# q before k in the first block, finer first transfers and a tile copied by two engines, in a fused attention and gMLP kernel

## The chip, the cores and the metric

The kernel runs on one core of a Trainium2 chip. The metric is the device time of one execution in microseconds (us). TensorE is called PE in the profile, VectorE DVE, ScalarE ACT, GpSimd POOL and SyncE SP.

## What is computed

The reference adds three things to one another for an input of 2048 tokens by 512 features in bf16: the input itself, a sliding local attention over eight earlier positions two tokens apart (32 heads of 16 features), and a gated MLP whose gate mixes all 2048 tokens by a matrix. Both branches start from the same layer norm of x.

```python
xn = _layernorm(x, axis=-1)
return x + _A_ref(xn, A_wqkv, A_wo) + _B_ref(xn, B_w_in, B_w_sp, B_b_sp, B_w_out)

# A: q, k, v = xn @ wqkv; logits over offsets 0, 2, ..., 14; softmax; weighted sum of v; @ wo
# B: z = gelu(xn @ w_in); z2 = layernorm(second half)
#    g = w_sp @ z2 + b_sp; (first half * g) @ w_out
```

## The kernel before

The tokens are cut into 16 tiles of 128. Tile i = 4 * tb + j belongs to block j, so that a block holds four tiles, one from each quarter tb of the sequence. In the code t0, i1, i2 and i3 are the tile numbers of blocks 0 to 3. Everything is kept in SBUF: `xall` holds x of all tiles and is normalised in place, `xnT` holds the normalised x with features on the partitions, `wqk` the weights of q (s = 0) and of k (s = 1), each in four chunks `kc` of 128 input features.

Each engine works through its instructions in the order in which the program text issues them: the schedule is written out by hand. The start of the kernel, with which the change deals, is plain code; after it a long string ORDER of tokens gives the order of all that follows (the gMLP's matmuls `z`, the remaining q and k, the products of the attention and so on).

At the start each tile goes through these steps:

- `ln_stats` (DVE): mean and variance by a statistics instruction and an aggregate. `ln_sqrt` (ACT): the square root of the variance plus epsilon, for one column or for a slice of several tiles' columns. `ln_recip` (DVE): its reciprocal. `ln_apply` (DVE): subtract and multiply in place. `ln_tile` is `ln_recip` and `ln_apply` of one tile.
- a transpose to `xnT`, in one of two ways: `tr` has PE write four 128 by 128 transposes to a PSUM tile `pt`, which `tr_copy` has ACT copy to `xnT`; `tr_dma` has SP issue a DMA transpose. Block 0 and two tiles of block 1 go by PE, the other tiles by DMA.
- q and k: `qk_part(pq, j, m, b0, b1)` has PE multiply the weights by tiles b0 to b1 of block j into the PSUM tile `pq`. m = 0 and 1 are the two halves of q, m = 2 and 3 those of k. `qk_copy` has ACT cast the result to SBUF.

The PSUM tiles of q, k and z come from one pool of three, `ps_mm`, so that a fourth tile waits until the first has been read. The `pt` tiles come from a pool of two, `ps_aux`.

x and the weights arrive by DMA. SP and ACT issue the first transfers: halves of the first two tiles of x on both, the other two tiles of block 0 on ACT, and on SP the q weights in two transfers of two chunks, x of block 1 in two transfers of two tiles, the k weights in one, then x of blocks 2 and 3 and the weights of z. In the built program all transfers share eight completion semaphores in turn.

Of the kernel before, what the change touches and what calls it, by code (L numbers as in the profile page):

```python
# [15 lines left out]
P = 128  # L16
# [3 lines left out]
TB = 4  # L20
TBS = 512
C = D // P
# [48 lines left out]
def kernel(  # L71
# [13 lines left out]
    V = nc.vector  # L85
# [3 lines left out]
    SP = nc.sync  # L89
# [3 lines left out]
    xblk = x2.rearrange("(b j p) d -> j p b d", b=TB, j=4)  # L93
# [9 lines left out]
    xall = r_x[:, 0:4 * TB * D].rearrange("p (j b d) -> p j b d", j=4, b=TB)  # L103
# [33 lines left out]
    xnT = sb.tile([P, C, S], BF16, name="xnT")  # L137
# [31 lines left out]
    def load_wqk(E, s, k0=0, k1=C):  # L169
        E.dma_start(wqk[:, s, k0:k1],  # L170
                    A_wqkv[:, s * D:(s + 1) * D].rearrange("(k p) f -> p k f", p=P)[:, k0:k1])
# [3 lines left out]
        load_x0(A, tb, 1)  # L175
    for tb in range(2, TB):
        A.dma_start(xall[:, 0, tb], xblk[0][:, tb])
    load_wqk(SP, 0, 0, 2)
    load_wqk(SP, 0, 2, 4)
    SP.dma_start(xall[:, 1, 0:2], xblk[1][:, 0:2])  # L180
    load_wqk(SP, 1)
    SP.dma_start(xall[:, 1, 2:4], xblk[1][:, 2:4])
    for j in range(2, 4):
        SP.dma_start(xall[:, j], xblk[j])
    SP.dma_start(w_z2[:], B_w_in[:, FH:F].rearrange("(k p) f -> p k f", p=P))
# [20 lines left out]
    def ln_stats(i, parts=1):  # L206
        j, tb = i % 4, i // 4
        w = D // parts
        for h in range(parts):
            V.bn_stats(stats[:, i, 6 * h:6 * h + 6], xall[:, j, tb, w * h:w * h + w])  # L210
        V.bn_aggr(mv[:, i, :], stats[:, i, 0:6 * parts])

    def ln_sqrt(sl):
        A.activation(rstd[:, sl], mv[:, sl, 1], ACT.Sqrt, bias=eps_t[:])

    def ln_recip(sl):
        V.reciprocal(rstd[:, sl], rstd[:, sl])

    def ln_apply(i):
        j, tb = i % 4, i // 4  # L220
        V.tensor_scalar(xall[:, j, tb, :], xall[:, j, tb, :], mv[:, i, 0:1], rstd[:, i:i + 1],
                        ALU.subtract, ALU.mult)

    def tr(i):
        j, tb = i % 4, i // 4
        pt = ps_aux.tile([P, C, P], BF16, name="pt", tag="aux")
        for c in range(C):
            PE.transpose(pt[:, c, :], xall[:, j, tb, c * P:(c + 1) * P], ident[:])  # L228
        return pt

    def tr_copy(i, pt, c0=0, c1=C):
        A.copy(xnT[:, c0:c1, i * P:(i + 1) * P], pt[:, c0:c1, :])

    def tr_dma(i):
        j, tb = i % 4, i // 4
        SP.dma_start_transpose(xnT[:, :, i * P:(i + 1) * P], xall[:, j, tb, :])
# [70 lines left out]
    def qk_part(pq, j, m, b0, b1, ccs=(0, 1), p0=None, kcs=range(C)):  # L307
        sd, c0 = m // 2, 2 * (m % 2)
        p0 = b0 if p0 is None else p0
        xv = xnT[:].rearrange("p k (b j t) -> p k b j t", b=TB, j=4)  # L310
        for cc in ccs:
            for kc in kcs:
                PE.matmul(pq[:, cc, p0 * P:(p0 + b1 - b0) * P], wqk[:, sd, kc, c0 + cc:D:C],  # L313
                          xv[:, kc, b0:b1, j, :], start=(kc == 0), stop=(kc == C - 1))

    def qk_copy(pq, j, m, b0=0, b1=TB, p0=None):
        sd, c0 = m // 2, 2 * (m % 2)
        p0 = b0 if p0 is None else p0
        if sd == 0:
            dst = qs[:, j, c0:c0 + 2, b0 * P:b1 * P].rearrange("p c (b t) -> p c b t", b=b1 - b0)  # L320
        else:
            dst = ks[:, c0:c0 + 2, HALO:HALO + S].rearrange("p c (b j t) -> p c b j t", b=TB, j=4)[:, :, b0:b1, j, :]
        cast = A.copy(dst, pq[:, :, p0 * P:(p0 + b1 - b0) * P].rearrange("p c (b t) -> p c b t", b=b1 - b0))  # L323
        if sd == 1:
            for i in k_reads[j]:
                tc.declare_no_dep(cast.ins, i, reason="other token columns of the same rows")
            k_casts[j].append(cast.ins)

    def qk_tile():
        return ps_mm.tile([P, 2, TBS], F32, name="pq", tag="mm")  # L330
# [214 lines left out]
    def blk(j):  # L545
        return [4 * tb + j for tb in range(TB)]

    def col(i):
        return slice(i, i + 1)
# [9 lines left out]
    def ln_tile(i):  # L559
        ln_recip(col(i))  # L560
        ln_apply(i)

    t0, i1 = blk(0), blk(1)
# [5 lines left out]
    for n in range(2):  # L569
        ln_tile(t0[n])  # L570
    tr_copy(t0[0], tr(t0[0]))
    pt1 = tr(t0[1])
    tr_copy(t0[1], pt1, 0, 2)
    tr_copy(t0[1], pt1, 2, 4)
    warm_up(1)
    warm_up(1, 2)
# [5 lines left out]
    pqs = [qk_tile() for _ in range(3)]  # L582
    qk_part(pqs[0], 0, 0, 0, 2, kcs=range(2))
    qk_part(pqs[0], 0, 0, 0, 2, kcs=range(2, 4))
    tr_copy(t0[2], tr(t0[2]))
    qk_part(pqs[1], 0, 1, 0, 2, (0,))
    tr_copy(t0[3], tr(t0[3]))
    qk_part(pqs[1], 0, 1, 0, 2, (1,))
    qk_part(pqs[2], 0, 2, 0, 2)
    for n in range(2):  # L590
        ln_stats(i1[n])
    ln_sqrt(slice(1, 8, 4))
    ln_stats(i1[2])
    ln_recip(slice(1, 8, 4))
    ln_apply(i1[0])
    ln_apply(i1[1])
    ln_stats(i1[3])
    for n in range(2):
        qk_part(pqs[n], 0, n, 2, 4)
        qk_copy(pqs[n], 0, n)  # L600
    ln_sqrt(slice(9, 16, 4))
    ln_stats(i2[0])
    ln_recip(slice(9, 16, 4))
    for n in range(2, 4):
        ln_apply(i1[n])
        tr_dma(i1[n])
    qk_part(pqs[2], 0, 2, 2, 4, (0,))
    tr_copy(i1[0], tr(i1[0]))
    qk_part(pqs[2], 0, 2, 2, 4, (1,))
    tr_copy(i1[1], tr(i1[1]))  # L610
    qk_copy(pqs[2], 0, 2)
    pq3 = qk_tile()
    qk_part(pq3, 0, 3, 0, 4)
    qk_copy(pq3, 0, 3)
    for n in range(1, 4):
        ln_stats(i2[n])
    ln_sqrt(blk_cols(2))
# [7 lines left out]
    pqs = [qk_tile() for _ in range(3)]  # L625
# [79 lines left out]
```

## Time and profile before

The times of six runs and the profiled execution:

| | us |
|---|---|
| median of six runs (lowest to highest) | 203.92 (203.46 to 204.85) |
| the profiled execution, time | 203.8 |
| the profiled execution, span in the trace | 201.9 |

So some 1.9 us of the time lie outside the span. The profile names the instructions by engine, line, operation, and output and input tiles. The page cuts the span into 40 equal slices and gives the busy share of each in tenths:

```profile
PE   7899999999999999999999999999999999999994
PEld 2689856655566666666556666666546645664562
DVE  5989799999999999999989998999999999999804
ACT  3575999999969983741742309546100210031000
POOL 3000000791000000000000000000000000000000
PEclk9999999999999999999999999999999999999999
```

A slice is about 5 us. PE is below nine tenths in the first two slices alone, apart from the last. In a list of waits, `<-` stands before what ended the wait. A timeline merges neighbouring instructions of one form: `x8` are eight of them, and the number in front is the start of the first. Ends of matmuls are modelled, so that neighbours overlap: the start of the next one tells when PE could go on.

### The profile page before, as it was taken

The page shows a single profiled execution, that of the slowest core. Times are in us where ns is not written, and L with a number is a line of the kernel's source. Part 1 is how long each engine was busy: PE and PEld are TensorE (multiplying, and loading weights), DVE is VectorE, ACT ScalarE, POOL GpSimd, SP SyncE. Part 2 cuts the span into 40 slices and gives each one's busy share as a digit, 9 for nine tenths or more (in the row PEclk, how much of TensorE's full clock was granted, in tenths as well). Part 3 has the DMA queues.
Part 4 walks back from the last instruction along what each step waited for, and adds up shares of the span by engine and source line. Part 5 has one row for each costly group of instructions (what it writes and reads, how often), then busy time and mean ns, then how long its engine had stood idle before and what let it go on. Part 6 is the DMA issues. An engine that isn't in the chain of part 4 may idle for free.

```text
span 201.9 us, 4038 instructions
## 1 busy us (share of the span) xinstructions
PE 196.5 (97%) x1671; PEld 124.7 (62%) x1675; DVE 187.0 (93%) x267; ACT 100.0 (50%) x162; POOL 11.5 (6%) x14
## 2 busy tenths in 40 slices
PE   7899999999999999999999999999999999999994
PEld 2689856655566666666556666666546645664562
DVE  5989799999999999999989998999999999999804
ACT  3575999999969983741742309546100210031000
POOL 3000000791000000000000000000000000000000
PEclk9999999999999999999999999999999999999999
DMA  5983447000498000696398966989916920744155
GB/s 165 331 270 74 96 92 248 0 0 0 95 170 157 3 0 0 124 240 129 70 180 202 197 164 105 208 171 159 205 24 175 227 49 0 221 98 94 50 161 177
DMA packets 66338, 25.91 MB, mean 128 GB/s; under 512 B 56272, under 2 KB 66064, under 8 KB 66064
## 3 DMA queue, kind: packets, MB, share of 16 engines
q1 hardware_dynamic: 65600, 25.19, 54.9%
q10 hardware_dynamic: 720, 0.47, 0.7%
q8 instruction: 13, 0.21, 0.4%
q14 instruction: 5, 0.04, 0.1%
HBM read 10.13 MB, written 2.10 MB: 61 GB/s over the span
## 4 chain that ended last, share of the span: by engine, by line
PE 92%; DMA 4%; DVE 1%; issue 1%; SPq 0%
PE pg L456 37%; PE pz L242 19%; PE pq L313 13%; PE po L529 7%; PE pv L417 7%; PE po L504 6%; DMA r_w<-in_A_wqkv_dram 3%; PE pl L367 1%; DMA r_x<-in_A_x_dram 1%; DVE r_pr L519 1%; PE po L513 1%; PE pb L504 1%; PE pa L313 0%; PE pt L228 0%; SPq L180 0%
## 5 line engine op out<-in xcount | busy, mean ns | idle before, releaser
L456 PE MATMUL pg<-z,r_qk 128*128 128x344 bf16 x448 | 67.3, 309 | 0.0
L456 PEld LDWEIGHTS <-r_qk 128*128 128x128 bf16 x448 | 43.7, 98 | 22.4 <-issue 0.8
L242 PE MATMUL pz<-w_z,xnT 128*128 128x344 bf16 x256 | 40.1, 309 | 0.0
L431 DVE TENSOR_TENSOR r_pr<-r_x,r_w 128x2048 bf16<-128x2048 bf16 x32 | 38.2, 1218 | 0.3
L435 DVE TENSOR_TENSOR r_pr<-r_pr 128x2048 bf16<-128x2048 bf16 x28 | 33.8, 1217 | 0.2
L462 ACT ACTIVATE gs<-pg,b_col 128x688 bf16<-128x688 f32 x16 | 13.3, 833 | 40.6 <-PE pg L456 25.1
L242 PEld LDWEIGHTS <-xnT 128*128 128x128 bf16 x256 | 24.9, 98 | 13.4 <-issue 0.8
L313 PE MATMUL pq<-xnT,r_w 128*128 128x256 bf16 (+1 forms) x176 | 28.9, 316 | 0.5 <-DMA r_w<-in_A_wqkv_dram 0.3
L347 DVE TENSOR_TENSOR r_pr<-r_qk 128x2048 bf16<-128x2048 bf16 x24 | 28.5, 1216 | 0.0
L313 PEld LDWEIGHTS <-r_w 128*128 128x128 bf16 x184 | 20.2, 114 | 7.7 <-DMA r_w<-in_A_wqkv_dram 0.6
L304 ACT ACTIVATE r_uz<-pz 128x688 bf16<-128x688 f32 x16 | 11.5, 742 | 22.5 <-PE pz L242 22.0
L323 ACT CAST r_qk<-pq 128x1024 bf16<-128x1024 f32 (+1 forms) x16 | 15.3, 988 | 2.4 <-PE pq L313 2.3
L529 PE MATMUL po<-r_w,r_uz 128*128 128x512 bf16 x66 | 14.9, 379 | 0.6 <-issue 0.6
L417 PE MATMUL pv<-xnT,r_w 128*32 128x512 bf16 x256 | 14.6, 380 | 0.0
L504 PE MATMUL po<-r_lg,r_pr 32*128 32x512 bf16 x224 | 14.5, 375 | 0.0
L529 PEld LDWEIGHTS <-r_uz 128*128 128x128 bf16 x85 | 8.0, 98 | 9.8 <-issue 1.5
L356 DVE TENSOR_TENSOR r_pr<-r_pr 128x4096 bf16<-128x4096 bf16 x6 | 13.7, 2282 | 0.0
L266 ACT ACTIVATE junk<-z 128x688 bf16<-128x688 bf16 x16 | 12.4, 778 | 0.2
L210 DVE BATCH_NORM_STATS2 stats<-r_x 128x6 f32<-128x512 bf16 (+1 forms) x18 | 10.9, 613 | 1.5 <-DMA r_x<-in_A_x_dram 1.5
L417 PEld LDWEIGHTS <-r_w 128*32 128x32 bf16 x256 | 9.5, 138 | 4.5 <-issue 0.3
L260 ACT ACTIVATE z<-pz 128x688 bf16<-128x688 f32 x16 | 11.8, 739 | 0.8 <-PE pz L242 0.8
L504 PEld LDWEIGHTS <-r_pr 32*128 32x128 bf16 x272 | 7.6, 93 | 6.5 <-issue 0.6
(82 smaller groups left out, 176.7 us busy)
## 6 DMA issues: line engine op xcount, KB each, us to landing
r_lg<-in_A_wo_dram SPq DMA_DIRECT2D x8, 256.0 KB, 4.0
r_qk<-in_A_x_dram SPq DMA_DIRECT2D x12, 128.0 KB, 2.2
out_dram<-r_qk SPq DMA_DIRECT2D x12, 128.0 KB, 2.1
w_z<-in_B_w_in_dram SPq DMA_DIRECT2D x2, 688.0 KB, 6.9
r_w<-in_A_wqkv_dram SPq DMA_DIRECT2D x2, 512.0 KB, 5.1
r_x<-in_A_x_dram SPq DMA_DIRECT2D x2, 512.0 KB
r_w<-in_B_w_out_dram SPq DMA_DIRECT2D x1, 640.0 KB, 5.6
r_w<-in_A_wqkv_dram SPq DMA_DIRECT2D x2, 256.0 KB, 4.3
```

The costliest lines, as they stand in the source:

```text
L242: PE.matmul(pz[:, hh, 0:FHALF], xnT[:, kc, i * P:(i + 1) * P], wz[:, kc, hh * FHALF:(hh + 1) * FHALF], start=(kc == 0), stop=(kc == C - 1))
L313: PE.matmul(pq[:, cc, p0 * P:(p0 + b1 - b0) * P], wqk[:, sd, kc, c0 + cc:D:C], xv[:, kc, b0:b1, j, :], start=(kc == 0), stop=(kc == C - 1))
L323: cast = A.copy(dst, pq[:, :, p0 * P:(p0 + b1 - b0) * P].rearrange("p c (b t) -> p c b t", b=b1 - b0))
L347: prod = V.tensor_tensor(pr[g % 3][:, c].rearrange("p w b t -> p b w t"), q3.unsqueeze(2).broadcast_to([P, TB, 4, P]), k4, ALU.mult)
L356: V.tensor_tensor(pr[g % 3][:, 0:2], pr[g % 3][:, 0:2], pr[g % 3][:, 2:4], ALU.add)
L417: PE.matmul(pv[32 * tb:32 * tb + 32, dd, :], wv[:, kc, 2 * d2 + dd, :], xnT[:, kc, tb * TBS:(tb + 1) * TBS], start=(kc == 0), stop=(kc == ...
L431: V.tensor_tensor(pw_t[n], vp[:, :, off:off + P], a_sb[:, slot_w(w), ts].unsqueeze(1).broadcast_to([P, DH, P]), ALU.mult)
L435: V.tensor_tensor(pw_t[n] if dst is None else dst, pw_t[n], pw_t[m], ALU.add)
L456: PE.matmul(pg[:, hh, 0:FHALF], wsp[n][:, k, :], z2[:, k, hh * FHALF:(hh + 1) * FHALF], start=(k == 0), stop=(k == NT - 1))
L462: A.activation(gs[:], tiles.pop(("g", n))[:, :, 0:FHALF], ACT.Identity, bias=b_col[:, i:i + 1])
L504: PE.matmul(pc, op[32 * tb:32 * tb + 32, d, o * P:(o + 1) * P], wo_r[32 * tb:32 * tb + 32, d, cs], start=(d == 8), stop=False, tile_positi ...
L529: PE.matmul(pc, uT[:, o % 2, m, tb * P:(tb + 1) * P], wout[:, m, cs], start=False, stop=(m == MCH - 3))
```

## The change

The k weights' first matmuls move behind q of all four tiles of block 0. The q weights come in four transfers of one chunk, x of block 1 in four transfers of one tile (the k weights between the second and the third). The PSUM tile of tile 3 of block 0 is copied in two halves, the first by DVE and the second by ACT. In block 1 the square roots are taken tile by tile, where before they were taken for two tiles at once, and casts, copies and statistics change their order accordingly: the casts of the two q tiles stand ahead of the roots of tiles 2 and 3 of block 1, and the first statistics of block 2 behind all of block 1. The k tile pqs[2] is written for all four tiles at once, and pq3 in two steps around the transposes of tile 1 of block 1.

```diff
@@ -175,11 +175,12 @@
-    load_wqk(SP, 0, 0, 2)
-    load_wqk(SP, 0, 2, 4)
-    SP.dma_start(xall[:, 1, 0:2], xblk[1][:, 0:2])
-    load_wqk(SP, 1)
-    SP.dma_start(xall[:, 1, 2:4], xblk[1][:, 2:4])
+    for kc in range(C):
+        load_wqk(SP, 0, kc, kc + 1)
+    for tb in range(TB):
+        if tb == 2:
+            load_wqk(SP, 1)
+        SP.dma_start(xall[:, 1, tb], xblk[1][:, tb])
@@ -230,6 +231,9 @@
+    def tr_copy_v(i, pt, c0, c1):
+        V.tensor_copy(xnT[:, c0:c1, i * P:(i + 1) * P], pt[:, c0:c1, :])
@@ -582,36 +586,36 @@
     pqs = [qk_tile() for _ in range(3)]
     qk_part(pqs[0], 0, 0, 0, 2, kcs=range(2))
     qk_part(pqs[0], 0, 0, 0, 2, kcs=range(2, 4))
+    qk_part(pqs[1], 0, 1, 0, 2, (0,))
     tr_copy(t0[2], tr(t0[2]))
-    qk_part(pqs[1], 0, 1, 0, 2, (0,))
-    tr_copy(t0[3], tr(t0[3]))
     qk_part(pqs[1], 0, 1, 0, 2, (1,))
-    qk_part(pqs[2], 0, 2, 0, 2)
+    pt3 = tr(t0[3])
+    tr_copy_v(t0[3], pt3, 0, 2)
+    tr_copy(t0[3], pt3, 2, 4)
+    qk_part(pqs[0], 0, 0, 2, 4, kcs=range(2))
+    qk_part(pqs[0], 0, 0, 2, 4, kcs=range(2, 4))
+    qk_part(pqs[1], 0, 1, 2, 4)
     for n in range(2):
         ln_stats(i1[n])
-    ln_sqrt(slice(1, 8, 4))
-    ln_stats(i1[2])
-    ln_recip(slice(1, 8, 4))
-    ln_apply(i1[0])
-    ln_apply(i1[1])
-    ln_stats(i1[3])
+        ln_sqrt(col(i1[n]))
     for n in range(2):
-        qk_part(pqs[n], 0, n, 2, 4)
+        ln_tile(i1[n])
         qk_copy(pqs[n], 0, n)
-    ln_sqrt(slice(9, 16, 4))
+    qk_part(pqs[2], 0, 2, 0, 4)
+    for n in range(2, 4):
+        ln_stats(i1[n])
+        ln_sqrt(col(i1[n]))
+    for n in range(2, 4):
+        ln_tile(i1[n])
+        tr_dma(i1[n])
+    tr_copy(i1[0], tr(i1[0]))
+    pq3 = qk_tile()
+    qk_part(pq3, 0, 3, 0, 4, (0,))
+    tr_copy(i1[1], tr(i1[1]))
+    qk_part(pq3, 0, 3, 0, 4, (1,))
+    qk_copy(pqs[2], 0, 2)
+    qk_copy(pq3, 0, 3)
     ln_stats(i2[0])
-    ln_recip(slice(9, 16, 4))
-    for n in range(2, 4):
-        ln_apply(i1[n])
-        tr_dma(i1[n])
-    qk_part(pqs[2], 0, 2, 2, 4, (0,))
-    tr_copy(i1[0], tr(i1[0]))
-    qk_part(pqs[2], 0, 2, 2, 4, (1,))
-    tr_copy(i1[1], tr(i1[1]))
-    qk_copy(pqs[2], 0, 2)
-    pq3 = qk_tile()
-    qk_part(pq3, 0, 3, 0, 4)
-    qk_copy(pq3, 0, 3)
     for n in range(1, 4):
         ln_stats(i2[n])
     ln_sqrt(blk_cols(2))
```

## The prediction

> **What bounds the kernel now.** I read the totals first, then PE's waits, then the chain of waits, then PE, ScalarE (ACT), VectorE (DVE) and SP in order of time up to 30 us. All times below are us from the span's start.
>
> The totals, and all that PE ever waited for (columns: who waited for whom, us, times, longest):
>
> ```profile
> PE 196.5 (97%) x1671; PEld 124.7 (62%) x1675; DVE 187.0 (93%) x267; ACT 100.0 (50%) x162; POOL 11.5 (6%) x14
> ...
> PE pwm L556 <- DVE warm L188: 1.1, 1, 1.1
> PE po L529 <- issue: 0.6, 4, 0.2
> PE pq L313 <- DMA r_w<-in_A_wqkv_dram: 0.3, 1, 0.3
> PE pt L228 <- DVE r_x L221: 0.2, 1, 0.2
> ```
>
> PE is the bound throughout. Only two of these waits lie where the change is: 0.2 for the normalised x of tile 2 and 0.3 for the k weights. The chain of waits shows the second:
>
> ```profile
> 3.42 6.22 DMA r_w<-in_A_wqkv_dram
> 9.64 0.05 issue
> 9.68 3.25 PE pq L313 x28
> ```
>
> From 9.68 to the store PE never stands for another engine, so a microsecond won or lost before 9.68 moves the end by as much, as long as PE finds its inputs ready.
>
> PE around that gap (start, us, count):
>
> ```profile
> 6.62 1.03 PE L313 MATMUL pq<-xnT,r_w 128*128 128x256 bf16 x8
> 7.88 0.40 PE L228 MATMUL pt<-ident,r_x 128*128 128x128 bf16 x4 [0.22 <-DVE r_x L221]
> 8.11 0.60 PE L313 MATMUL pq<-xnT,r_w 128*128 128x256 bf16 x4
> 8.55 0.39 PE L228 MATMUL pt<-ident,r_x 128*128 128x128 bf16 x4
> 8.77 0.60 PE L313 MATMUL pq<-xnT,r_w 128*128 128x256 bf16 x4
> 9.68 3.25 PE L313 MATMUL pq<-xnT,r_w 128*128 128x256 bf16 x28 [0.31 <-DMA r_w<-in_A_wqkv_dram]
> ```
>
> A 256-column matmul takes one slot of 0.110 (28 fill 9.68 to 12.77), so the four from 8.77 leave PE free at 9.21 and the hole is 0.47. ACT and SP there:
>
> ```profile
> 8.31 1.25 ACT L232 COPY xnT<-pt 128x512 bf16<-128x512 bf16 x2 [0.66 <-PE pt L228]
> 13.47 0.31 ACT L214 ACTIVATE rstd<-mv,eps_t 128x2 f32<-128x2 f32 x1
> 13.67 1.07 ACT L232 COPY xnT<-pt 128x512 bf16<-128x512 bf16 x2
> 14.62 1.98 ACT L323 CAST r_qk<-pq 128x1024 bf16<-128x1024 f32 x2
> ...
> 3.42 0.47 SPq L170 DMA_DIRECT2D r_w<-in_A_wqkv_dram  x1
> 3.93 0.51 SPq L182 DMA_DIRECT2D r_x<-in_A_x_dram  x1
> ```
>
> **What the Trainium skill says.** "VectorE: DVE Perf Modes", the errata section: a PSUM read costs (120 + columns/mode) cycles at 0.96 GHz; for 256 columns an estimated 0.39 at one, 0.26 at two per cycle. No such copy is in this trace; DVE's 512-column add from PSUM (L519, 0.69) agrees with the form (0.66). "PSUM — Partial Sum Buffer", the section on bank collisions: accesses of two engines to one bank must be kept apart, reads too. No run here shows it; in the changed program ACT's half copy of tile 3 does wait for DVE's half. "DMA: Bandwidth & Descriptors": transfers issued from several engines share the same 16 DMA engines and interleave, and HBM gives about 358 GB/s to a core. The trace agrees: 349 to 382 GB/s in each microsecond from 8 to 13.
>
> **The change, part by part.** *q ahead of k.* Before 9.68 PE now does the same work as before: 16 matmuls and both transposes. pqs[0] starts at 6.62 as before (it waits for ACT's copies of tile 1) and ends at 7.50, the half of pqs[1] at 7.94; the transposes of tile 2, ready since 7.88, follow without the 0.22 wait to 8.17, the other half of pqs[1] to 8.61, the transposes of tile 3 (x ready at 8.33) to 8.84. PE is done 0.37 earlier than at 9.21, but next come q of tiles 2 and 3, which need tile 3 copied. The k weights are needed 16 matmuls later.
>
> *Tile 3 by halves.* In the trace a copy starts 0.43 after its transposes (7.88 to 8.31), so DVE's half starts at 9.04. I take 0.35 (between 0.26 and 0.39, close to ACT's 0.37 for such a half): done 9.39, PE restarts at 9.45. ACT's half follows, 9.44 to 9.81, just ahead of the second four matmuls at 9.89. PE restarts 0.23 before 9.68. What waits behind the copy on DVE is block 1: its statistics began at 8.25 and now begin at 9.34.
>
> *Finer transfers.* In the built program all transfers use eight completion semaphores in turn, and the ninth waits for the first (the trace has two such waits of SP for x: 0.3 ahead of L180, 0.2 ahead of the second L184). Three more transfers shift who waits for whom. The third and fourth quarter of the q weights wait for the first x halves (landed near 2.95) and go out near 3.0 and 3.4, not 2.2; they are needed at about 7.1. 64 KB took 2.0 to 2.2; 256 KB under the full queue 4.3, which gives 5.5 to 7.7; I take 6.5, no wait, and keep 0.6 as the bad end. The k weights now wait for x of tile 2 (landed near 5.15, by the second L184) and go out at 5.2 instead of 3.42. Bytes ahead of them are unchanged and the queue was full, so they should land near 9.7 to 10.2. At worst 5.2 + 6.2 = 11.4. PE needs them at 9.45 + 16 x 0.110 = 11.21. x of block 1 goes out last at about 6.3 (behind x of tile 3) and lands by 10.5 to 11.5, at worst 6.3 + 6.4 = 12.7; DVE wants it at 12.8.
>
> *DVE and ACT of block 1, root by root.* DVE pair of statistics and aggregate 0.80, reciprocal 0.17, apply 0.33 from start to start. DVE from 9.34: two pairs to 10.97, two reciprocals and applies to 11.99, pairs of tiles 2 and 3 to 13.61, their applies to 14.61. ACT: roots 10.29 and 11.09, casts of pqs[0] and pqs[1] from 11.29 and 12.21, roots 13.13 and 13.73, then what stood behind the roots: copies of tiles 0 and 1 from 13.93 and 14.46 (before 13.67 and 14.14), done 15.05, casts of pqs[2] to 15.93 and pq3 to 16.85 (before 16.60).
>
> PE: 16 matmuls to 11.21, pqs[2] as 8 of 512 columns (0.216 each, no dearer than 16 of 256) to 12.94, transposes, half of pq3 to 14.03, transposes, other half to 15.12. Block 1 begins at 15.12 (before 15.38) and needs tile 1 copied: 15.05 plus 0.06. Its second tile needs pqs[2]'s bank at 16.00: free at 15.99. Its third needs pq3's at 16.88: free at 16.91. So all three just fit; PE begins pa3 at 17.80 instead of 18.00: gain 0.20. The two DMA transposes of block 1 go out at 14.2 and 15.4 (before 14.46 and 15.86), before PE wants them.
>
> *What is late next.* DVE reaches the applies of block 2 at 18.79 instead of 18.06, because it stood for the copy. SP's four transposes of block 2 (1.27 apart, 2.4 to landing) then start at 19.24 instead of 18.50; the last lands at 25.5. PE wants it at 25.67 (before 25.87): 0.2 of cover. The 1.17 that DVE stood at 21.85 for the root of block 3 absorbs the rest: statistics end at 22.6, that root falls at 22.6 as before, and DVE begins its products near 24.5 again. Later cover is larger: the first logits at 44.53 read what DVE finished at 42.65, the first gate product at 76.06 what it finished near 74.9. So PE's gain passes.
>
> *Sum.* Hole 0.47 and wait 0.22 go, a new stand of 0.61 (8.84 to 9.45) comes, with rounding 0.03 at the third bank: 0.2 less. The profiled execution has span 201.9 and time 203.8 (1.9 around it), 0.1 under the median of 203.92. On the median: 203.7. The cap is what PE idles after 6.62, under 0.7.
>
> **Rivals.** (1) *The k weights still end the wait:* they land at the bad end 11.4, PE stands 0.2, and the gain is gone: 203.9. For it: SP issues them 1.8 later. Against: the queue had at least 0.4 MB in front at 5.2.
> (2) *DVE's stand is paid in blocks 1 and 2:* the copy costs more than 0.39, or a root misses its slot; the two copies, two casts and SP's transposes all move, with no cover. 0.4 late is 0.2 lost: 204.1. For it: four fits within 0.2. Against: each duration is from a row.
> (3) *The eight semaphores starve the queue (slower):* while SP stands for x of tile 2 and 3, nothing is issued; the DMA already fell to 181 GB/s from 6.4 to 7.3. A hole of 1.2 on top of the bad ends puts the k weights at 12.6 and the last x at 13.9; PE loses 1.4 at pqs[2] less 0.25: 205.0. It decides from a landing later than 11.45. Against: 1.28 MB are issued before the first such stand, and only 0.8 MB had moved by 5.
>
> **How the numbers follow.** Gain as worked out 0.50 (203.7, own range 203.3 to 203.9); (1) 0.14; (2) 0.17; (3) 0.19. The bound for faster, same and slower is 0.5%, about 1.0 us, what a measurement can tell. Faster 0.04 (the cap is below it, only scatter remains). Slower: most of (3) and a little of (2), 0.18. Same 0.78. Low 203.3 is the cheap copy plus scatter (0.05 below), high 204.7 leaves out most of (3).
>
> **What would show it.** Right: PE's hole moves to 8.8 to 9.4 and its releaser is the DVE or ACT copy, no DMA wait in front of pqs[2], block 1 begins near 15.1, q of block 2 near 25.7 without a wait. Wrong: a wait on the weights at 7.1 or 11.2, ACT copies of block 1 later than 14.5, a DMA wait of DVE's statistics after 12, or a PE wait for a transposed tile of block 2.

## The result, and the profile after

| | us |
|---|---|
| changed, median of 35 runs (lowest to highest) | 204.43 (203.91 to 205.08) |
| before on the same chip, median of 72 runs | 204.61 (203.34 to 205.99) |
| ratio changed to before | 1.0000, 95% interval 0.9988 to 1.0011 |
| the changed kernel's profiled execution, time and span | 204.26 and 202.4 |

The ratio comes from the measurement with its interval and is not the quotient of the two medians, so that the two can point different ways. The two kernels can't be told apart here: the interval runs from 0.25 us less to 0.22 us more, and so does not exclude the 0.2 us of gain that was forecast. Two later comparisons, on two chips, gave 1.0022 (1.0008 to 1.0035) and 1.0036 (1.0023 to 1.0049), and these exclude it. So the change is worth nothing that shows, or costs some 0.2 to 0.4%. Between the three comparisons it is mostly the kernel before that differs: its medians are 204.61, 204.29 and 203.76, those of the changed kernel 204.43, 204.60 and 204.75. Its executions scatter widely; 42 of 72 lie above 204.4 in the first comparison, 8 of 35 in the last.

The waits of PE in the changed kernel (who waited for whom: us, times, longest):

```profile
PE pq L317 <- DVE xnT L236: 0.4, 1, 0.4
PE pq L317 <- DMA xnT<-r_x: 0.4, 1, 0.4
PE pq L317 <- ACT xnT L233: 0.2, 1, 0.2
```

The wait for the k weights is gone. The first line is the stand for tile 3's copy, which the prediction had. The second is new and was not expected: q of block 1 waits for a tile that SP's DMA transpose brings. PE in order of time (start, us, what):

```profile
6.89 1.47 PE L317 MATMUL pq<-xnT,r_w 128*128 128x256 bf16 x12 [0.19 <-ACT xnT L233]
...
8.85 0.39 PE L229 MATMUL pt<-ident,r_x 128*128 128x128 bf16 x4
9.63 3.67 PE L317 MATMUL pq<-xnT,r_w 128*128 128x256 bf16 x24 [0.39 <-DVE xnT L236]
...
17.98 1.04 PE L317 MATMUL pa<-xnT,r_w 128*128 128x256 bf16 x8
19.39 3.68 PE L317 MATMUL pq<-xnT,r_w 128*128 128x256 bf16 x32 [0.37 <-DMA xnT<-r_x]
```

`pa` (pa3 of the prediction) is the last PSUM tile of the first half of block 1. Its eight matmuls fill 0.87, so PE is free at 18.85 and stands to 19.39: a hole of 0.54 (the 0.37 of the line counts from the modelled end of the matmuls). In the kernel before the same instructions follow one another without a hole (list up to 20):

```profile
18.00 1.04 PE L313 MATMUL pa<-xnT,r_w 128*128 128x256 bf16 x8
18.87 1.36 PE L313 MATMUL pq<-xnT,r_w 128*128 128x256 bf16 x11
```

All that follows `pa` has nearly one length: from the start of its successor (19.39 here, 18.87 before) the profiled time ends 184.87 and 184.93 later, and 184.75 to 184.95 later in all other traces but four, which come up below. So that one start tells a run's time, as long as nothing happens in the tail. The chain of waits of the changed kernel names what PE stood for:

```profile
15.73 3.61 DMA xnT<-r_x
19.34 0.05 issue
19.39 2.70 PE pq L317 x23
```

The second of the two transposes of block 1 goes out at 15.73, about when the one before did (15.86), and lands 3.61 later instead of 2.4. The first, issued at 14.34, takes 4.5 instead of 2.5. In the kernel before the list of DMA issues from 16 to 19, with the second of block 1 and the first of block 2, has (median us from issue to landing, at the end):

```profile
xnT<-r_x SPq DMA_TRANSPOSE x2, 2.4
```

### The profile page after: what moved, and what is told of

Same layout as the page of the kernel before. It is cut to its first block, busy times and chain, and to the rows that moved or that the text cites. A ratio compares the mean times of both kernels' runs of the same rounds, so it can differ in the third digit from the quotient of the medians.

```text
span 202.4 us, 4028 instructions
## 1 busy us (share of the span) xinstructions
PE 196.9 (97%) x1663; PEld 124.4 (61%) x1667; DVE 187.5 (93%) x270; ACT 100.4 (50%) x164; POOL 12.6 (6%) x14
## 4 chain that ended last, share of the span: by engine, by line
PE 91%; DVE 4%; DMA 2%; issue 1%; ACT 0%
PE pg L460 37%; PE pz L246 19%; PE pq L317 10%; PE po L533 7%; PE pv L421 7%; PE po L508 6%; PE pwm L560 2%; DMA xnT<-r_x 2%; DVE stats L211 2%; PE pl L371 1%; DVE r_pr L523 1%; DVE r_x L222 1%; PE po L517 1%; PE pb L508 1%; DVE mv L212 0%
## 5 line engine op out<-in xcount | busy, mean ns | idle before, releaser
L317 PEld LDWEIGHTS <-r_w 128*128 128x128 bf16 x176 | 19.3, 114 | 8.9 <-DMA xnT<-r_x 0.6
L533 PE MATMUL po<-r_w,r_uz 128*128 128x512 bf16 x66 | 14.9, 379 | 0.6 <-issue 0.6
L421 PE MATMUL pv<-xnT,r_w 128*32 128x512 bf16 x256 | 14.6, 380 | 0.0
L650 POOL CAST b_col<-b 128x16 f32<-128x16 bf16 x1 | 10.6, 10593 | 33.4 <-DMA b<-in_B_b_sp_dram 33.4
```

What stands on the lines that cost most here:

```text
L421: PE.matmul(pv[32 * tb:32 * tb + 32, dd, :], wv[:, kc, 2 * d2 + dd, :], xnT[:, kc, tb * TBS:(tb + 1) * TBS], start=(kc == 0), stop=(kc == ...
L533: PE.matmul(pc, uT[:, o % 2, m, tb * P:(tb + 1) * P], wout[:, m, cs], start=False, stop=(m == MCH - 3))
```

## What holds the transposes up: the theories

*A: late bulk.* The finer first transfers push the weights and x back, so that other traffic is under way when the transposes go out. *B: the order itself*, whatever the transfers do. (Where an expectation below names a rival in another way, its own words say what it holds.) *D, formed after the first four runs: PE's own instructions.* The page's table of DMA queues for the changed kernel lists, beside the data (queue, kind: packets, MB, share):

```profile
q8 instruction: 13, 0.21, 0.4%
```

PE has 1663 matmuls and 1667 weight loads in this trace; 0.21 MB over 3330 instructions are 63 bytes each, and 0.21 MB over 13 packets are 16 KB, some 256 instructions, each. So q8 looks like PE's instruction stream, a packet for every 128 matmuls with their loads. Such a packet falls into this stretch in every trace. In the kernel before, the DMA queues in the window 14.25 to 14.30 show it,

```profile
q8 instruction: 1, 0.02, 116.0%
```

and in the changed kernel those from 16.55 to 16.60:

```profile
q8 instruction: 1, 0.02, 143.6%
```

The share is of 16 engines' time in 0.05 us, 0.8 us in all: the one packet takes 0.93 and 1.15 us, presumably on one engine. Before, it starts just ahead of the two transposes (14.46 and 15.86). Now it starts in the middle of them. The rate of all DMA in 40 slices of 0.2 us from 13 to 21, before and then changed, shows what that does:

```profile
GB/s 372 351 296 186 131 83 144 48 21 0 0 0 0 38 218 219 166 15 0 0 133 223 216 84 0 41 0 0 0 0 0 0 0 83 225 219 126 3 0 6
```

```profile
GB/s 389 399 391 386 419 368 370 372 303 255 220 165 103 208 233 224 98 100 13 22 178 212 175 30 9 50 10 10 0 0 0 0 0 0 0 0 0 22 207 220
```

Each hump of some 200 is one transpose. Before, the second hump falls to nothing at 17.8, and the tile has landed by 18.3. In the changed kernel the second hump (17.0 to 17.8) is followed by 9 and 10 GB/s from 17.8 to 18.6. (The 41 and 50 at 18.0 are in both kernels: an 8 KB packet of another instruction queue, q14, which starts at 18.1 to 18.2 in both and so is not what differs.) These 9 and 10 are a small rest that is worked off after all else is done. The packets of the trace, taken singly, show it too: 13 of the small ones of 256 or 4 bytes, whose median is 0.02 us, start between 17.5 and 17.7, take 0.8 to 1.0 and end together at 18.5, 0.8 after q8's packet. In the kernel before none takes over 0.5. The two transposes land only behind that rest, at 18.8 and 19.3.

Why the packet moved: the change writes pqs[2] in 8 matmuls of 512 columns, where 16 of 256 did it, so PE needs 8 matmuls and 8 loads fewer ahead of block 1, and the 256th instruction comes later. Theory D therefore says that the number of PE instructions ahead decides, and nothing else in the change.

## The experiments

All runs; "packet" is the start of q8's packet in this stretch, "landing" the longer time from issue to landing of block 1's two transposes, "hole" PE's stand after pa, all of the profiled execution. Packet starts are the lower edge of the short window that showed the packet. There is one profile per run, and those of e2, e5 and e8 are of the fastest of their 22 executions. The runs from one "before" in the column of medians to the next were made together, on one chip, and share that kernel before.

| run | edit | packet | landing | hole | median | ratio (95%) |
|---|---|---|---|---|---|---|
| e0 | before | 14.35 | 2.4 | 0 | 204.00 (before 203.83) | 1.0006 (0.9982 to 1.0029) |
| e1 | changed, old transfers | 17.35 | 4.1 | 1.01 | 204.75 | 1.0039 (1.0024 to 1.0054) |
| e2 | before, finer transfers | 13.95 | 2.6 | 0 | 204.49 | 1.0026 (1.0013 to 1.0038) |
| e3 | changed, second half of w_z late | 17.50 | 4.3 | 1.25 | 205.06 | 1.0044 (1.0024 to 1.0065) |
| e5 | changed, k in 256 columns | 14.2 | 2.6 | 0 | 204.01 (before 203.95) | 1.0009 (0.9992 to 1.0026) |
| e6 | changed, +15 warm-ups | 14.8 | 3.3, issued 0.7 late | 0.87 | 203.99 | 0.9999 (0.9975 to 1.0022) |
| e7 | e5, copy by ACT alone | 14.7 | 3.6 | 0 | 204.10 | 1.0003 (0.9987 to 1.0019) |
| e8 | e5, old transfers | 14.2 | 2.6 | 0 | 203.93 | 0.9985 (0.9968 to 1.0002) |
| e9 | before, pqs[2] in 512 columns | 16.1 | 4.5 | 1.26 | 205.25 (before 204.29) | 1.0050 (1.0024 to 1.0075) |
| e10 | changed | 16.5 | 4.1 | 0.91 | 204.60 | 1.0022 (1.0008 to 1.0035) |
| e11 | changed, +27 warm-ups | 13.6 | 2.6 | 0 | 204.07 | 0.9984 (0.9967 to 1.0001) |
| e12 | e8 | 14.6 | 3.3, issued 0.7 late | 0.84 | 203.89 | 0.9979 (0.9964 to 0.9994) |
| e13 | e1, +27 warm-ups | 14.4 | 2.7 | 0 | 204.30 (before 204.02) | 1.0012 (0.9988 to 1.0036) |
| e14 | before, +27 warm-ups | 14.1 | 2.5 | 0 | 204.60 | 1.0024 (1.0007 to 1.0041) |
| e15 | e11 | 14.0 | 2.6 | 0 | 204.29 | 1.0012 (0.9996 to 1.0027) |
| e16 | e8 | 13.2 | 2.5 | 0 | 203.84 (before 203.76) | 0.9997 (0.9983 to 1.0012) |
| e17 | changed | 16.8 | 3.9 | 0.82 | 204.75 | 1.0036 (1.0023 to 1.0049) |

The packet column sorts the holes: none where it starts at or before 14.4 and in e7, and one of 0.5 to 1.3 in every trace where it starts from 16.1 to 17.5 (0.54 in the changed kernel's first profile). Between, at 14.6 to 14.8, it starts within the first transpose, and of three such traces two have a hole. In the third, e7, the landing was late too, but the transposes had gone out 0.6 and 0.7 earlier than in e5, at 13.79 and 15.19, and PE did not stand: a late landing costs only what exceeds its cover, the time between a landing and the moment at which PE wants it. The slow small packets stand in seven traces, the changed kernel's first and e1, e3, e7, e9, e10 and e17: 6 to 15 of them, which all end 0.8 to 0.9 after q8's packet.

Whether the count or the time sets the packet can be read from the traces. When it starts, PE has begun 163 to 213 matmuls and weight loads in all 19 of them (a few records can be missing). e9 has 173 where the kernel before has 175, though the packet comes 1.85 later; e11, with 54 more in the stream, has 201 where e10 has 189, and the packet comes 2.8 earlier. So it is the count, but only roughly: three traces of one program (e8, e12, e16) have 179, 191 and 163, and e14, which has 54 more in the stream than the kernel before, has 209.

**Which part of the change: e0, e1, e2.** e1 takes back the finer transfers, e2 makes them alone:

```diff
-    for kc in range(C):
-        load_wqk(SP, 0, kc, kc + 1)
-    for tb in range(TB):
-        if tb == 2:
-            load_wqk(SP, 1)
-        SP.dma_start(xall[:, 1, tb], xblk[1][:, tb])
+    load_wqk(SP, 0, 0, 2)
+    load_wqk(SP, 0, 2, 4)
+    SP.dma_start(xall[:, 1, 0:2], xblk[1][:, 0:2])
+    load_wqk(SP, 1)
+    SP.dma_start(xall[:, 1, 2:4], xblk[1][:, 2:4])
```

> The kernel before once more, unchanged, for its scatter: the trace shown of it was at 203.8, the median of its many runs is 204.6, while the changed kernel's runs lie close together. Theory A: another execution of it stands longer for the k weights than the 0.47 of the trace shown (by up to 1 us), or starts its transposes on a slower PE clock (0.3). Rival B: it scatters in a late stage. Ratio 1.000 by construction.

> The new order of compute with the old first transfers (q weights in two, x of block 1 in two, k weights between). Theory A (the finer transfers make SP stand at its completion semaphores, the bulk of x and w_z then ends some 1.8 us later and the DMA transposes of block 1 land behind it, so that PE stands about 0.5 us after pa3): the second transpose of block 1 lands 2.4 us after its issue as before, the hole after pa3 goes, and the time is 0.4 to 0.7 us below that of the changed kernel, ratio to before 0.996 to 0.998. Rival B (the transposes of block 1 are late because the new order on DVE and ACT issues them late): the hole stays and the ratio is 1.000. Rival C (nothing at the start matters beyond the scatter of PE's clock there): ratio 1.000 whatever the trace shows.

> The old order of compute with the finer first transfers. Theory A: the k weights go out near 5.5 instead of 3.4 and land near 11 us, where the old order wants them at 9.2, so PE stands some 1.5 us there, and the transposes of block 1 land late as well but behind that; ratio 1.005 to 1.010. Rival B: the finer transfers do nothing by themselves, ratio 1.000 (0.998 to 1.002).

With the old transfers (e1) the hole is not gone but 1.01; with the finer ones in the old order (e2) the transposes land in 2.6. So the transfers are not the cause, and theory A falls. The order gains what it should in e1: pq to pa takes 11.09, as in the changed kernel, against 11.41 in e0. e2's median is 0.66 above its kernel before, and its one profile (203.83) shows no reason; in the new order the finer transfers made no difference that can be told (medians of e5 beside e8 204.01 and 203.93, of e15 beside e13 204.29 and 204.30; the ratios of e5 and e8 lie further apart, but their intervals overlap).

**Other traffic: e3.** The last big transfer is issued behind the two transposes:

```diff
-    SP.dma_start(w_z2[:], B_w_in[:, FH:F].rearrange("(k p) f -> p k f", p=P))
     ...
+    SP.dma_start(w_z2[:], B_w_in[:, FH:F].rearrange("(k p) f -> p k f", p=P))
```

> The changed kernel with the load of w_z2 (688 KB) issued behind the two DMA transposes of block 1 instead of ahead of them. Theory A: nothing large is in flight when the transposes go out near 14.3 and 15.7, they land within 2.4 to 2.6 us, the hole of about 0.5 after pa3 goes, and w_z2 lands near 20 to 21.5, ahead of its use near 22.5: ratio 0.996 to 0.998. Rival B (the transposes are late by themselves, or x of blocks 2 and 3 alone fills the queue): the hole stays, ratio 1.000. Third way: w_z2 lands after 22.5 and PE stands for it by as much as it is late.

The transposes then start on a nearly idle DMA and yet the second takes 4.3, the hole 1.25. This is the second refutation of A, and it turned the search to the other thing in the queues, the instruction packets. (Other traffic does delay a transpose: here the first two of block 2, issued beside w_z2, took 3.7 and 3.0. But it is not what delays those of block 1.)

**PE's instruction count: e5 to e8.** e5 writes both k tiles in 256 columns, 16 matmuls and 16 loads more than the changed kernel; the time of the matmuls is the same. e6 puts 20 warm-ups of 128 columns in place of five of 512; e7 is e5 with tile 3 copied whole by ACT; e8 is e5 with the transfers of before.

```diff
-    qk_part(pqs[2], 0, 2, 0, 4)
+    for b in (0, 2):
+        qk_part(pqs[2], 0, 2, b, b + 2)
...
-    qk_part(pq3, 0, 3, 0, 4, (0,))
+    for b in (0, 2):
+        qk_part(pq3, 0, 3, b, b + 2, (0,))
...
-    qk_part(pq3, 0, 3, 0, 4, (1,))
+    for b in (0, 2):
+        qk_part(pq3, 0, 3, b, b + 2, (1,))
```

```diff
-    warm_up(10)
+    warm_up(5)
+    warm_up(20, 1)
```

> The changed kernel with the k tiles of block 0 in 32 matmuls of 256 columns instead of 16 of 512 (0.110 against 0.216 each, so PE's work is the same to 0.05 us, but PE's instruction stream is 32 instructions longer there). Theory D (PE's instructions come in packets of 16 KB, 256 instructions; one such packet keeps one DMA engine for about 1 us; in the changed order it falls at 16.6 to 17.5 us, into the two DMA transposes of block 1, whose last part then lands 1.2 to 1.9 us late and PE stands for it): the packet moves ahead of the transposes, to 14 to 15, they land after 2.4, the hole after pa3 goes, and the time is 0.4 to 0.9 below the changed kernel's, ratio to before 0.996 to 0.999 on this scale where the changed kernel is 1.000 to 1.003. Rival B (the transposes land late for the way the new order issues them): the hole stays at 0.4 to 1.1 and nothing changes.

> The changed kernel with its ten warming matmuls at the start cut finer: five of 512 and twenty of 128 columns instead of ten of 512, the same columns in 30 more instructions; nothing else is touched. Theory D: the packet of 16 KB again falls ahead of the transposes of block 1, the hole after pa3 goes, 0.4 to 0.9 below the changed kernel unless PE's clock rises later for the finer matmuls. Rival B: the hole stays. Rival E (it was the shape of the k matmuls that mattered in the other run): the hole stays here and goes there.

> As the run with k in 256 columns, and tile 3 copied whole by ACT, none by DVE. It tells what the split copy is worth once the transposes land in time. Theory of the prediction: ACT's whole copy of 0.59 takes 0.3 longer than DVE's half, so PE restarts 0.2 to 0.3 later; DVE no longer stands for it and starts block 1 some 0.8 to 1.2 earlier, which PE does not need: 0.2 to 0.3 slower than the run with k in 256 columns. Rival: block 1 on DVE and ACT is what PE waits for, and the two are equal or this one is faster.

> As the run with k in 256 columns, with the old first transfers (q weights in two, x of block 1 in two). It tells what the finer transfers are worth once the transposes land in time. If they only delay SP: 0 to 0.2 faster than with the finer ones. If the x or weights come earlier by them: 0.1 to 0.3 slower.

In e5's profile the packet comes at 14.2, the transposes land in 2.5 to 2.6 and the hole is gone. That execution was the fastest; 9 of the 22 took over 204.5, and whether they had the hole is not shown. e6 moved the packet less far than meant, to 14.8, and its profile has a hole of 0.87 in another form: the second issue came at 16.49, some 0.7 late, and then landed in 3.3. Its median, 203.99, lies below that profiled execution's 204.59; so most of its executions probably had less of it. e7 against e5 prices the split copy: PE restarts at 9.93, not 9.63, and pa starts at 18.27, not 18.01. On the medians (204.10 and 204.01) this is not to be seen.

**The cause alone: e9, e10, e11.** e9 puts the smaller PE count into the kernel before, by writing pqs[2] in 512 columns, which also moves its first half behind q; e10 is the changed kernel again; e11 leaves everything of the change and puts 36 warm-ups of 128 columns in place of nine of 512:

```diff
-    qk_part(pqs[2], 0, 2, 0, 2)
...
-    qk_part(pqs[2], 0, 2, 2, 4, (0,))
+    qk_part(pqs[2], 0, 2, 0, 4, (0,))
...
-    qk_part(pqs[2], 0, 2, 2, 4, (1,))
+    qk_part(pqs[2], 0, 2, 0, 4, (1,))
```

```diff
-    warm_up(10)
+    warm_up(1)
+    warm_up(36, 1)
```

> The kernel before, with the k tile pqs[2] written by 8 matmuls of 512 columns behind q of all four tiles, instead of 16 of 256 in two parts: 16 instructions fewer in PE's stream, everything of DVE, ACT and the transfers as before, so that the transposes of block 1 go out at 14.4 and 15.9 as before. Theory D: PE's packet of 16 KB now falls at 16 to 17.5 as in the changed kernel, into those transposes; the second lands 3.3 to 4.3 after its issue instead of 2.4, and PE stands 0.4 to 1.1 after pa3, where the kernel before never stood; ratio 1.001 to 1.005. Rival B (the transposes land late because the changed order of DVE and ACT, or the finer transfers, issue them so): they land after 2.4 as before, no hole, ratio 0.998 to 1.000.

> The changed kernel, unchanged, on the same chip as the other three: a second trace of it. Theory D: the packet at 16 to 17.5 again, a hole of 0.4 to 1.1 after pa3, ratio 1.000 to 1.004, and 0.3 to 0.6 us above the two runs that move the packet away.

> The changed kernel with the ten warming matmuls cut into one of 512 and 36 of 128 columns: 54 instructions more at the very start, everything behind them untouched. Theory D: the packet falls near 11 to 12 us, far ahead of the transposes of block 1, which then land 2.4 to 2.6 after their issue; no hole after pa3; 0.3 to 0.6 below the changed kernel on the same chip. In the cut with 30 instructions more it had come at 14.8 and still lay over the first transpose. Rival B: the hole stays.

> The changed order of compute with k in 256 columns and the old first transfers, once more, on the same chip as the changed kernel: the candidate for the best version. Packet at 14 to 14.3, no hole after pa3, 0.3 to 0.7 below the changed kernel, ratio to before 0.997 to 1.000.

e9 makes the kernel before ill: the chain of waits has the second transpose,

```profile
16.16 4.47 DMA xnT<-r_x
```

and the DMA rate from 16 to 19, in slices of 0.075, shows a rest being worked off alone, mostly at 7 to 10 GB/s, from 17.3 to 18.1, before the second transpose's hump starts at 18.4:

```profile
GB/s 38 365 198 218 201 208 201 208 143 59 11 0 0 0 0 0 0 7 7 10 10 7 10 10 10 7 10 21 7 0 0 27 119 218 195 222 212 188 215 304
```

Here SP's second issue lasted 2.20 instead of 1.2. Not all of e9's loss is the hole of 1.26: pa comes 11.71 after pq, 0.3 later than before, since PE stood 0.6 for a tile of x and 0.2 for a copy. e11 cures the changed kernel on the chip on which e10 had a hole of 0.91; PE in order of time (start, us, what):

```profile
18.17 1.04 PE L317 MATMUL pa<-xnT,r_w 128*128 128x256 bf16 x8
19.04 3.66 PE L317 MATMUL pq<-xnT,r_w 128*128 128x256 bf16 x32
```

Neither the order, nor the transfers, nor the 512 columns of k differ between e10 and e11, only the shape of the warm-ups and so how many instructions PE has behind it; pa comes 11.09 after pq in both. e12, the program of e8 again, had an execution profiled in which the packet came at 14.6 and a hole of 0.84 stood, though its median was the best of all against its kernel before; that execution, 204.55, was the slowest but one of 22. The packet's start is thus not fixed by the program: 14.2, 14.6 and 13.2 in three traces of this one.

**A failed forecast of theory D: e13, e14, e15.** The warm-ups of e11 in e1's program, in the kernel before, and e11 again:

> The new order of compute, the old first transfers, and the warming matmuls cut into one of 512 and 36 of 128 columns (54 more PE instructions at the start). Theory D: the packet comes near 12 to 13.6, ahead of the transposes of block 1; no hole after pa3 in any run; the 0.3 that the new order gains before pa3 reaches the end: ratio to before 0.996 to 0.998, with the runs close together. If instead the finer transfers were worth something, it is slower than the same with finer transfers by 0.1 to 0.3.

> The kernel before with the warming matmuls cut in the same way, nothing else. In its traces the packet lies at 14.2 to 14.4, with the first transpose of block 1 issued at 14.5 to 14.9. Theory D for its scatter (203.4 to 205.3): in part of its executions the packet comes a little later and lies over the transposes, as in the second trace of the candidate with k in 256 columns (14.6, hole 0.7). Then moving the packet to about 11 to 12.5 takes the upper half of its times away: median 0.2 to 0.5 lower, ratio 0.997 to 0.999. Rival F (its scatter comes from the k weights or from the rise of PE's clock): the scatter and the median stay, ratio 0.999 to 1.001.

> The changed kernel with the warming matmuls cut so, once more beside the other two on one chip: ratio 0.997 to 1.000, no hole after pa3. It is equal to the same with old transfers within 0.2 if the finer transfers only move waits that nothing waits for.

No trace of the three has the hole, and yet none is faster than the kernel before; e14 is 0.58 slower. The packet came later than forecast, too, at 14.0 to 14.4 and not at 11 to 13.6: more instructions move it ahead, but how far was not foreseen. Two things had been left out. The first shows in e14's waits, and its size in the chain:

```profile
PE pq L313 <- DMA r_w<-in_A_wqkv_dram: 1.3, 1, 1.3
```

```profile
3.38 7.41 DMA r_w<-in_A_wqkv_dram
```

In the old order the k weights' landing scatters: 9.64, 10.04 and 10.79 in the traces of before, e0 and e14, for the same issue at 3.4. The second is a collision of the same kind at the other end of the kernel. The 54 instructions that the warm-ups add move every later packet, the last one too. In the chain of e15,

```profile
190.23 4.33 DMA r_uz<-r_uz
```

the kernel's last DMA transpose takes 4.33, with a packet at 192.5, and PE stands for it; e13 (4.27) and e14 (4.16) show the same. The packet comes at the very end of the transfer: 30 of 32 writes of 4 bytes that close the transpose are done by 192.4, and the last two, a sixteenth, as one engine of 16 would have, come at 194.2 and 194.55. In e11, the same program, all 32 lie ahead of the packet, and the tail has its usual length, 184.77. In the kernel before, the transpose goes out at 190.19, the packet comes at 193.3, and PE does not wait. From pa's successor the profiled times end 185.39, 185.42 and 185.26 later in e15, e13 and e14, 0.3 to 0.6 more than the 184.75 to 184.95 of the other traces (the fourth exception is e16, below). So what theory D says of the hole stands, its forecast of the times failed, and e11's good ratio was not a property of that edit: e15 is the same program.

**Side by side: e16, e17.** The program of e8 and the changed kernel, 14 and 22 runs:

> The program of e8 a third time: the changed order with the first transfers of the kernel before and the k tiles in 256-column matmuls. Theory D (a 16 KB packet of PE's instructions holds one DMA engine for about 1 us and delays a transpose that it meets): the packet lies near 14.2 to 14.8, just ahead of the two transposes, so the hole after pa3 is absent in most executions, and the order's 0.29 us stand: 203.6 to 204.0, ratio to the kernel before 0.997 to 0.9995, and 0.4 to 0.8 us under e17 on the same chip. A rival, that the two earlier ratios (0.9985 and 0.9979) were luck of the draw, expects 1.000 to 1.002 and no difference from e17.

> The changed kernel a third time, beside e16. Theory D: packet at 16.4 to 16.7, the second transpose of block 1 lands 3.5 to 4.2 after its issue, a hole of 0.35 to 0.8 after pa3; 204.3 to 204.7, ratio 1.000 to 1.003. The rival: no different from e16.

203.84 against 204.75: 0.91 between them, by the traces a hole of 0.82 against none, with pa 11.12 and 11.09 after pq. e16 has a longer tail, 185.18 from pa's successor: there an issue of SP, for a load of x, lasts 2.30 beside a packet at 192.6, as the chain shows:

```profile
192.55 2.30 SPq L484
```

That the earlier ratios were luck is refuted in so far as the two programs differ, but not beside the kernel before: of 0.9985, 0.9979 and 0.9997 only the second has an interval that excludes 1. No version tried here beat the kernel before in more than one comparison.

## Why the prediction was right and wrong

The median fell into the range and into the likeliest class. That was luck and a wide range (203.3 to 204.7): the kernel before measured 204.61 beside it and not the 203.92 of the sum, and the gain that the sum carries to the end was lost on the way. Of its steps those on PE, DVE and ACT held, and one on the DMA did not.

The sum as written does not give its own result: 0.47 + 0.22 - 0.61 - 0.03 is 0.05, not 0.2. Its 0.22 counts from the modelled end of the matmuls. In slots of 0.110, which the 0.47 uses, PE was free at 7.50 and stood to 7.88, so 0.38; with that the sum is 0.21, as the account part by part has it, and the cap is 0.85, not under 0.7.

- *The gain up to pa: right.* From pq's start to pa: 11.38 before, 11.09 changed, 0.29 less, where 0.20 was forecast. The absolute times stand 0.2 later because pq started at 6.89; it was at 6.62 in the trace of before, which is the earliest of all traces (6.69 to 7.09 in the others).
- *The copy by halves: right.* The Trainium skill, "VectorE: DVE Perf Modes", errata section, left 0.39 or 0.26 open; the copy took 0.29, near the form with two columns per cycle, so the 0.35 of the forecast was a little dear. From DVE's timeline, and then from ACT's, the two halves; the second waits for the first:

```profile
9.28 0.29 DVE L236 COPY xnT<-pt 128x256 bf16<-128x256 bf16 x1 [0.81 <-PE pt L229]
```

```profile
9.60 0.37 ACT L233 COPY xnT<-pt 128x256 bf16<-128x256 bf16 x1 [0.40 <-DVE xnT L236]
```

- *The weights (rivals 1 and 3): right that they don't decide, but by less than forecast.* The k weights went out at 5.48 (forecast 5.2) and landed at 10.94 (forecast 9.7 to 10.2), 0.45 before PE reached them at 9.63 + 16 x 0.110 = 11.39; in e6 it was 11.41, 0.07 before. The queue was not full, as the forecast had it: 282 to 306 GB/s in each microsecond from 8 to 12, where the kernel before had 349 to 382 (so the 358 that the prediction quotes is no ceiling here). What the reckoning missed is that in the old order the landing scatters into PE's way: 9.64 and 10.04 in two traces of the kernel before, 10.79 in e14, where PE wanted them near 9.2. The new order wants them some 2 us later and takes most of that chance away.
- *Block 1's roots, copies and casts (rival 2): right.* ACT's copies began at 14.05 (forecast 13.93), and block 1 began, and reached pa, without a stand.
- *"The two DMA transposes of block 1 go out at 14.2 and 15.4 (before 14.46 and 15.86), before PE wants them": this step failed.* They went out at 14.34 and 15.73, but the landing was carried over from the trace before at 2.4, and took 4.5 and 3.6. The prediction looked at DVE, SP's queue and the landing of block 2's transposes, and did not reckon the cover of those of block 1: by its own numbers PE wants the second at 17.80 + 0.87 = 18.67, 3.3 after its issue, which is 0.9 over the 2.4; in the trace it was 18.85 - 15.73 = 3.1, and 0.7. What used it up was the packet of PE's instructions, which the change itself moved from 14.25 to 16.55 by saving 16 of them. The saved instructions had been entered at nothing ("no dearer than 16 of 256"). This took 0.54 from the 0.29 in the first profile, and 0.8 to 0.9 in e10 and e17.
- *Block 2 onwards: right.* Its transposes started at 19.38 (forecast 19.24), and q of block 2 came without a wait, at 26.41 (forecast 25.67: the hole of 0.54 and the later start make up the difference).

Left open: why a packet sometimes delays SP's issue and sometimes the rest of a transpose; which engine of the 16 it takes, and why the transpose's share ends not with the packet but 0.8 to 0.9 later; whether the slower executions of the kernel before and of e5, none of which was traced, are late weights, the hole or both; and what e2's median lost.

## What to carry to other kernels

A transfer that lands just in time is a risk even if the queues look empty: write down the cover of every DMA that the next stage needs, here 0.7 us, and hold it against the scatter of such landings, not against one trace's median. An edit that changed how many instructions PE has also moved the moments at which its instruction packets came, so test such an edit against the same edit with the count restored, and look at the whole kernel: a packet that leaves one transfer can meet another, as in the tails of e13 to e16. Where two versions differ by a few tenths of a microsecond, run them on the same chip and look at more than one trace of each.

## What the runs showed of the hardware

A packet of q8, 16 KB, PE's instructions by the count above, took 0.9 to 1.3 us in this stretch of the 19 traces. A DMA transpose of one 128 by 512 tile, 2.4 to 2.6 us from issue to landing if alone, was late when such a packet started 0.4 us or more after the first of a pair went out: the slower of the two took 3.3 to 4.5. In seven traces it left a mark of its own, some 10 GB/s for 0.6 to 1 us after the hump, which ended 0.8 to 0.9 after the packet; in e6 and e12 it was SP's issue that lasted longer, 2.0 instead of 1.3. More PE instructions ahead brought the packet earlier (16 to 54 more: at 13.2 to 14.9 in place of 16.1 to 17.5). The same k-weight load of 512 KB, issued at 3.4 with the same bytes ahead, landed 6.2, 6.6 and 7.4 us later in three traces.
